# Early x sums, a slot table for the Sinkhorn iterations and an expert-major product, in an attention and mixture-of-experts kernel

## The chip, the cores and the metric

The kernel runs on one core of one Trainium2 chip. The metric is the device time of one execution in microseconds (us). A core has five engines with instruction queues of their own: TensorE (PE; its weight loads are listed as PEld), VectorE (DVE), ScalarE (ACT), GpSimd (POOL) and SyncE (SP), which here only issues DMAs. Each executes its queue in order. An instruction that needs the result of another engine waits for a semaphore, and all that is queued behind it on its engine waits too.

## The reference

```python
k_p, q_p = phi(k), phi(q)      # relu times cos and sin of the position
kv = einsum('bhsf,bhsd->bhfd', k_p, v); z = k_p.sum(2)
x = (q_p @ kv) / (q_p . z + 1e-6)          # 8 batches x 576 rows -> [4608, 512]
P = exp(x @ w_gate)                        # [4608, 8 experts]
for _ in range(8):                         # Sinkhorn
    P /= P.sum(1, keepdims=True) + 1e-9
    P /= P.sum(0, keepdims=True) + 1e-9
    P *= N / E
for e in range(8):
    out += P[:, e:e+1] * (relu(x @ w1[e]) @ w2[e])   # w1 512 x 1024, w2 1024 x 512
```

## The kernel before

**Attention and expert 0, blocks 0 to 6.** x is kept transposed in SBUF as `xT` (128 partitions, 4 slabs of 128 features, 4608 tokens, 16 bit). Expert 0 is computed plainly in blocks of 512 tokens. A block has 16 slots (`NS`): in slots 0 to 7 `ffn1` makes one 128-feature slice of the hidden layer (4 matmuls on PE, relu on ACT), in slots 8 to 15 `ffn2` makes half of a 128-row output tile (4 matmuls; ACT or DVE then copies the tile into the accumulators `acc`). Beside block j the attention of batch j+1 is made: a hand-written list (`todo`, filled by `at(block, slot, ...)`, L587 to L728) says after which slot each step is issued. In block 6 those are `sums` (slot 0), `denominators` (3), `gates` (5) and `attend` (6, 8, 10, 12) of batch 7. `attend` multiplies on DVE into `xT`; `den` and `hl` are the denominators on DVE.

**Blocks 7 and 8** (L1096 to L1121). Attention is over, its pools are closed and their SBUF is used again (weights `wB` of expert 1, hidden layer `H`, `S`, `T` tiles). `gates` of the last batch (L1110) completes the table `P_tok` (128 partitions, 36 token groups, 8 experts, f32). From here on DVE runs the Sinkhorn iterations, a generator (`sinkhorn`, L1022) that `balanced(n)` (L1057) moves on by n steps. Each iteration has five steps: row sums `rs` and their reciprocal `rr`; P_tok times rr and the column sums `colp`; two of the weight sums `T` of expert 1; a matmul of colp with ones, the **Sinkhorn product** (it sums over partitions; the profile's `copied_ps<-colp,ones_all`), and further weight sums; reciprocal `t` and the scaling of P_tok. Block 8 makes its `ffn1` only; its output tiles are left to the unit that follows.

**Experts 1 to 7** use a Strassen-Winograd scheme (7 products for a 2x2 block matrix). Tokens are cut into 6 units of 2 x 384; `group` (L867) makes one slice of the hidden layer of a unit from 7 products of two matmuls each (0.33 us a product) in the PSUM banks X (`h_ps`), Y (`copied_ps`) and Z (`p7_ps`). ACT copies X to Y and takes snapshots u2 and u4 of X; DVE adds them to Z with `add_relu` (L853, in the trace CUSTOM_DVE_ANT_0). The last product of a group is put off into the next group (`late`). Each group calls `fill()` seven times between its products. In the first unit (e = 1, n = 0) the fill is `start_fill` (L1146): it adds pieces of block 8's output tiles (two matmuls) and `balanced` steps. Two matmuls called marks (L1014) enclose this unit: the profile's `copied_ps<-xT`, at 188.79 us and 209.97 us. After it the gates' P values are final, ACT and POOL scale the accumulators, and from then on the fill is the second layer of the unit before.

**x sums.** The scheme needs sums of x blocks for each unit: `x_sums(n)` (L803), four DVE instructions of 128x768 in place S1, S2, S4 and a part of `xT` itself. The three S tiles are also saved to DRAM by SP (L814, `x_saved`), and later experts load them again (`x_again`, L816). Units 0 and 1 are made in blocks 7 and 8, one instruction after a slot (L1112 to L1116).

**Order.** During all of this DVE, ACT and PE execute in written order (`InOrder`, L101). SP and POOL execute in the order in which their instructions were placed.

Of the kernel before, what the change touches and what calls it, by code (L numbers as in the profile page):

```python
# [25 lines left out]
def kernel(  # L26
# [128 lines left out]
    def ffn2(hT, w, c0, g, y_ps, fts):  # L155

        for ft in fts:
            te.matmul(
                out=y_ps,
                lhsT=hT[:, ft, c0 : c0 + P],  # L160
                rhs=w[1][:, ft, :],
                start=(ft == 0),
                stop=(ft == FT - 1),
            )
        if FT - 1 in fts:

            if g % 2 == 0 or g < (B - 1) * TCH // P:
                se.copy(out=acc(g), in_=y_ps)
            else:
                ve.tensor_copy(out=acc(g), in_=y_ps)  # L170

    def store(g, cols=slice(0, Dm), queues=(nc.sync, nc.sync)):
        for half, queue in enumerate(queues):
            w_ = 2 * g + half
            b, c = w_ // C, w_ % C
            rows = out[b * S : (b + 1) * S].rearrange("(p c) d -> p c d", c=C)
            queue.dma_start(
                out=rows[:, c, cols], in_=acc(g)[half * HP : (half + 1) * HP, cols]
            )

    with ExitStack() as p1:
        ld = p1.enter_context(tc.tile_pool(name="ld", bufs=4))
# [404 lines left out]
        def at(block, slot, fn, *args):  # L587
            todo.setdefault((block, slot), []).append((fn, args))
# [62 lines left out]
        for j in range(B):  # L651
# [70 lines left out]
            if j == 1:  # L722
                for name in "qkv":
                    for half in range(2):
                        at(j, 12, load, b + 2, half, name, True)
            elif j and b + 2 < B:
                for half in range(2):
                    at(j, 11 + half, load, b + 2, half, "qkv", True)  # L728
        y_pss = {}
        for j in range(B - 1):  # L730
            if j:
# [34 lines left out]

    NT = N // 2
    TU = 3 * P  # L770
    NU = NT // TU
    KH = KT // 2
    FH = FT // 2
    UG = TU // P
    DH = Dm // 2
    w_next = load_weights(wB, 1)

    H = hB.tile([P, 2, FT, 2 * TU], F16, name="H")
# [12 lines left out]
    Y = ps_k.tile([P, TCH], FP32, name="copied_ps")  # L791
    Z = ps_k.tile([P, TCH], FP32, name="p7_ps")

    def x_part(half, kh, n):
        t0 = half * NT + n * TU
        return xT[:, kh * KH : (kh + 1) * KH, t0 : t0 + TU]

    x_saved = dram.tile([NU, 3, P, KH * TU], F16, name="x_saved")

    def x_tiles():  # L800
        return [s2_pool.tile([P, KH, TU], F16, name=name) for name in ("S1", "S2", "S4")]

    def x_sums(n, ts):  # L803

        a11, a12, a21, a22 = (x_part(i, j, n) for i in range(2) for j in range(2))
        s1, s2, s4 = (t[:] for t in ts)
        for out_, in0, in1, op in (
            (s1, a21, a22, ALU.add), (s2, s1, a11, ALU.subtract),
            (s4, a12, s2, ALU.subtract), (a21, a11, a21, ALU.subtract),
        ):  # L810
            ve.tensor_tensor(out=out_, in0=in0, in1=in1, op=op)
            yield
        for i, t in enumerate(ts):
            nc.sync.dma_start(out=x_saved[n, i], in_=t[:].rearrange("p k t -> p (k t)"))  # L814

    def x_again(n, ts):  # L816
        for i, t in enumerate(ts):
            nc.sync.dma_start(out=t[:].rearrange("p k t -> p (k t)"), in_=x_saved[n, i])
# [203 lines left out]
    def sinkhorn():  # L1022

        total = W2[:, 0:E]
        for it in range(8):
            rs = sk_pool.tile([P, NG], FP32, name="rs")
            ve.reduce_sum(out=rs[:], in_=P_tok[:], axis=AX.X)
            rr = sk_pool.tile([P, NG], FP32, name="rr")
            ve.reciprocal(out=rr[:], in_=rs[:])
            yield  # L1030
            ve.tensor_tensor(
                out=P_tok[:], in0=P_tok[:],
                in1=rr[:].unsqueeze(2).to_broadcast([P, NG, E]), op=ALU.mult,
            )
            colp = sk_pool.tile([P, E], FP32, name="colp")
            ve.reduce_sum(
                out=colp[:], in_=P_tok[:].rearrange("p c e -> p e c"), axis=AX.X
            )
            yield
            for step in tw_steps[it][:2]:  # L1040
                step()
            yield
            te.matmul(out=total, lhsT=ones_all[:], rhs=colp[:], start=True, stop=True)
            for step in tw_steps[it][2:]:
                step()
            yield
            t2 = sk_pool.tile([P, E], FP32, name="t2")
            ve.reciprocal(out=t2[:], in_=total)
            ve.scalar_tensor_tensor(
                out=P_tok[:], in0=P_tok[:],  # L1050
                scalar=float(N) / float(E) / (XS if it == 7 else 1.0),
                in1=t2[:].unsqueeze(1).to_broadcast([P, NG, E]),
                op0=ALU.mult, op1=ALU.mult,
            )
            yield

    def balanced(steps):  # L1057
        for _ in range(steps):
            next(balance, None)
# [26 lines left out]

    balance = sinkhorn()

    tws, tw_steps = [], [[] for _ in range(8)]
    for i in range(FH):  # L1090
        tw, tw_steps[1 + i] = w1_steps(w_next, i)
        tws.append(tw)
    xs_first = [x_tiles() for _ in range(2)]
    xs_next = xs_first[0]
    sums_x = x_sums(0, xs_next)
    for j in range(B - 1, NJ):  # L1096
        hT = next_h()
        tiles = dealt(
            hT, w0, [(ts * P, j * TCH // P + ts) for ts in range(TCH // P)],
            2 if j < NJ - 1 else 4,  # L1100
        )
        for slot in range(NS):
            if slot < FT:
                ffn1(hT, w0, j, [slot])
            elif j < NJ - 1:
                next(tiles)
            else:
                break
            if j == B - 1 and slot == 0:
                gates(B - 1, Z[:])  # L1110
            if j == B - 1 and slot:
                next(sums_x, None)  # L1112
            if j == NJ - 1:
                if slot == 0:
                    sums_x = x_sums(1, xs_first[1])
                next(sums_x, None)  # L1116
            since = (j - B + 1) * NS + slot - 5
            if since == -4:
                balanced(3)
            elif since >= 0 and since % 5 < 2:  # L1120
                balanced((1, 4)[since % 5])  # L1121


    OFFSETS = {"P1": 0, "P2": 3, "P7": 4, "P6": 5, "P4": 8, "P5": 9, "P3": 13}
# [21 lines left out]
    def start_fill():  # L1146

        nonlocal k_fill
        if k_fill % 7 in (0, 2, 3, 5):
            next(tiles, None)  # L1150
        if k_fill % 6 != 1:
            balanced(1)
        k_fill += 1

    def pair_fill():
# [11 lines left out]
    for e in range(1, E):  # L1167
        if e == 2:
            se = nc.scalar
        w = w_next  # L1170
        for n in range(NU):
            hT = next_h()
            xs = xs_next
            for i in range(FH):
                group(hT, tws[i], xs, n, i, start_fill if e == 1 and n == 0 else pair_fill)
                m = (n + 1) % NU
                if e == 1 and m:

                    if n == 0:
                        xs_next = xs_first[1]  # L1180
                        continue
                    if i == 0:
                        xs_next = x_tiles()
                        sums_x = x_sums(m, xs_next)
                    next(sums_x)
                    if i == FH - 1:
                        next(sums_x, None)
                elif i == 1:
                    xs_next = x_tiles()
                    if not (e == E - 1 and m == 0):  # L1190
                        x_again(m, xs_next)

                if e > 1 and n == 0 and i == 0:
                    tws[FH - 1] = w1_sums(w, FH - 1)
                if e + 1 < E and n == NU - 1:
                    if i:
                        tws[i - 1] = w1_sums(w_next, i - 1)
                    else:
                        w2_first(w_next)
            if e == 1 and n == 0:  # L1200
                k_fill = 0
                for _ in tiles:
                    pass
                for _ in balance:
                    pass
                mark(W2[:])
                w2_first(w)
                for _ in range(2):
                    gate(ungated.pop(0), nc.gpsimd)
                ve = nc.vector  # L1210
            if n == 0 and e + 1 < E:
                w_next = new_weights(wA if e % 2 else wB)
                load_w1(w_next, e + 1, 1)
            if n == 2 and e + 1 < E:
                load_w2(w_next, e + 1, 1)
            add_pairs(hT, e, w, n)
# [36 lines left out]
```

The softmax here doesn't subtract the row's maximum and nothing guards it: scores larger than these inputs give would overflow.

## Time and profile before

| what | us |
|---|---|
| median of 6 runs | 981.71 (980.59 to 983.95) |
| profiled execution, whole | 981.78 |
| its span, first to last instruction | 980.1 |
| PE, DVE, ACT busy | 964.5, 806.9, 564.4 |
| a slot of `ffn1` or `ffn2`, from start to start | 0.87 |
| `rs`, `rr`, P_tok times rr, `colp`, `t`, scaling (one each) | 0.45, 0.38, 0.46, 0.67, 0.20, 0.46 |
| one instruction of x sums | 0.55 |
| one weight sum T | 0.28 |
| first Sinkhorn product, last one | 172.15, 204.01 |

All times within the execution count from the start of the span. A busy time is from the start to the end of an instruction. Matmuls overlap: two of them at 128x384 are listed with 0.49 us, and the next pair starts 0.33 us after them. DVE instructions overlap a little too, when one does not need the other: an x sum of 0.55 us is followed 0.47 us after its start. The clock granted to PE was 0.999 of full speed.

### The profile page before, as it was taken

The numbers are of one execution on the slowest core, as the hardware profiler recorded it, in microseconds if no ns is written. First come the engines' busy times: TensorE is split into PE (matmuls) and PEld (weight loads), VectorE is DVE, ScalarE is ACT, GpSimd is POOL, SyncE is SP. The second block draws the span as 40 slices with busy tenths as digits, with TensorE's granted clock in tenths as the row PEclk, the third lists the DMA queues.
The fourth block names the chain that finished last, engine by engine and source line by source line (L and its number), as shares of the span: only waits on it lengthen the run. The fifth ranks groups of instructions, "written<-read, shape, count | busy, mean of one in ns | idle before, by whom it ended". The sixth has DMA issues, their size and how long they took to land.

```text
span 980.1 us, 20237 instructions
## 1 busy us (share of the span) xinstructions
PE 964.5 (98%) x7855; PEld 673.9 (69%) x7855; DVE 806.9 (82%) x1833; ACT 564.4 (58%) x1262; POOL 60.7 (6%) x82
## 2 busy tenths in 40 slices
PE   9999999999999999999999999999999999999997
PEld 6544454457777777777777777777777777777775
DVE  6767774888988888988888888988888888988887
ACT  5766655467776555555555555555555555555551
POOL 6231110010000000000000000000000000000001
PEclk9999999999999999999999999999999999999999
DMA  9999885330113400223103401223103401104435
GB/s 164 183 147 178 149 143 95 79 73 25 43 32 68 92 26 25 64 57 66 49 25 70 91 25 32 61 56 69 42 25 76 85 25 35 40 26 120 127 88 128
DMA packets 80336, 73.54 MB, mean 75 GB/s; under 512 B 33264, under 2 KB 72176, under 8 KB 80240
## 3 DMA queue, kind: packets, MB, share of 16 engines
q0 software_dynamic: 27232, 30.94, 20.3%
q1 hardware_dynamic: 52768, 41.06, 16.9%
q8 instruction: 61, 1.00, 0.4%
q14 instruction: 35, 0.29, 0.1%
q10 hardware_dynamic: 240, 0.26, 0.1%
HBM read 83.12 MB, written 12.98 MB: 98 GB/s over the span
## 4 chain that ended last, share of the span: by engine, by line
PE 88%; DMA 5%; DVE 3%; issue 2%; ACT 1%; POOL 1%; POOLq 0%; ACTq 0%; SPq 0%
PE rows_ps L109 33%; PE h_ps L109 26%; PE p_ps L109 11%; PE copied_ps L109 11%; PE y_ps L109 4%; PE small_ps L109 3%; DMA k_ld<-in_k_dram 1%; DMA w1e<-in_moe_w_dram 1%; DMA w2e<-in_moe_w_dram 1%; DMA acc_hi<-q_p 1%; DVE P_tok L109 1%; DVE colp L109 0%; POOL q_ld L202 0%; DVE rs L109 0%; DVE acc_hi L926 0%
## 5 line engine op out<-in xcount | busy, mean ns | idle before, releaser
L926 DVE SCALAR_TENSOR_TENSOR acc_lo<-rows_ps,P_tok,acc_lo 128x512 f32<-128x512 f32 (+1 forms) x322 | 203.2, 639 | 75.0 <-PE rows_ps L109 74.9
L109 PEld LDWEIGHTS <-H 128*128 128x128 f16 x2080 | 203.0, 98 | 82.6 <-issue 1.2
L862 ACT CAST u<-h_ps 128x384 f16<-128x384 f32 x288 | 137.6, 478 | 131.2 <-PE h_ps L109 131.2
L109 PEld LDWEIGHTS <-w1e 128*128 128x128 f16 x1632 | 157.3, 98 | 67.4 <-issue 5.7
L856 DVE CUSTOM_DVE_ANT_0 H<-p_ps,u 128x384 f16<-128x384 f32 x329 | 180.9, 550 | 6.5 <-PE p_ps L109 6.5
L109 PEld LDWEIGHTS <-hs 128*128 128x128 f16 x1500 | 146.5, 98 | 56.2
L109 PE MATMUL h_ps<-S,w1e 128*128 128x384 f16 x672 | 164.2, 326 | 0.7 <-ACT u L109 0.6
L109 PE MATMUL p_ps<-xT,T 128*128 128x384 f16 x672 | 164.1, 326 | 0.1
L109 PE MATMUL rows_ps<-V,H 128*128 128x256 f16 x1000 | 150.0, 273 | 0.7 <-DVE acc_hi L926 0.7
L109 PE MATMUL rows_ps<-w2e,hs 128*128 128x256 f16 x1000 | 150.0, 273 | 0.0
L109 PE MATMUL h_ps<-xT,w1e 128*128 128x384 f16 (+1 forms) x616 | 149.4, 350 | 0.1
L894 ACT ACTIVATE H<-h_ps 128x384 f16<-128x384 f32 x144 | 70.6, 490 | 95.1 <-PE h_ps L109 95.1
L109 PEld LDWEIGHTS <-T 128*128 128x128 f16 x1008 | 98.4, 98 | 29.9 <-issue 3.2
L109 PE MATMUL rows_ps<-w2e,H 128*128 128x256 f16 (+1 forms) x568 | 92.3, 285 | 0.0
L875 ACT COPY copied_ps<-h_ps 128x384 f32<-128x384 f32 x144 | 67.5, 469 | 35.3 <-PE h_ps L109 35.3
L885 ACT ACTIVATE H<-copied_ps 128x384 f16<-128x384 f32 x144 | 70.8, 492 | 20.4 <-PE copied_ps L109 20.4
L109 PE MATMUL h_ps<-S,T 128*128 128x384 f16 x336 | 81.8, 325 | 0.3 <-ACT copied_ps L109 0.3
L109 PE MATMUL copied_ps<-xT,w1e 128*128 128x384 f16 x336 | 82.1, 326 | 0.0
L109 PE MATMUL copied_ps<-w2e,H 128*128 128x256 f16 x504 | 75.5, 272 | 0.0
L109 PE MATMUL rows_ps<-V,hs 128*128 128x256 f16 x500 | 75.0, 273 | 0.0
L926 DVE SCALAR_TENSOR_TENSOR acc_lo<-copied_ps,P_tok,acc_lo 128x256 f32<-128x256 f32 x126 | 60.0, 476 | 0.4
L926 DVE SCALAR_TENSOR_TENSOR acc_hi<-rows_ps,P_tok,acc_hi 128x512 f32<-128x512 f32 (+1 forms) x56 | 41.3, 737 | 20.5 <-PE rows_ps L109 19.7
(145 smaller groups left out, 948.2 us busy)
## 6 DMA issues: line engine op xcount, KB each, us to landing
S<-x_saved SPq DMA_DIRECT2D x108, 192.0 KB, 2.3
out_dram<-acc_lo SPq DMA_DIRECT2D x62, 128.0 KB, 2.4
w1e<-in_moe_w_dram POOLq DMA_DIRECT2D x7, 1024.0 KB, 8.7
w2e<-in_moe_w_dram POOLq DMA_DIRECT2D x7, 1024.0 KB, 9.8
q_ld<-in_q_dram POOLq DMA_DIRECT2D x16, 288.0 KB, 6.5
k_ld<-in_k_dram POOLq DMA_DIRECT2D x16, 288.0 KB, 8.4
v_ld<-in_v_dram POOLq DMA_DIRECT2D x16, 288.0 KB, 9.7
x_saved<-S SPq DMA_DIRECT2D x18, 192.0 KB, 1.9
```

The costliest lines, as they stand in the source:

```text
L109: i = getattr(self.engine, name)(*args, **kwargs)
L856: latest = ve._custom_dve(TENSOR_ADD_SAT, out=out, in0=ps[:, 0:TU], in1=t[:], s0=FP32_MAX, s1=0.0)
L862: se.copy(out=t[:], in_=ps[:, 0:TU])
L875: se.copy(out=Y[:, 0:TU], in_=X[:, 0:TU])
L885: se.activation(out=h11, in_=Y[:, 0:TU], func=AF.Relu)
L894: se.activation(out=h12, in_=X[:, 0:TU], func=AF.Relu)
L926: ve.scalar_tensor_tensor(out=a, in0=rows, scalar=P_tok[:, g, self.e : self.e + 1], in1=a, op0=ALU.mult, op1=ALU.add,)
```

## The change

1. **x sums of units 0 and 1** are made in block 6, after slot 1 and slot 8, into tiles of the pool of `k_p`, which are free by then (`x_sums_early`). SP saves them to `x_saved`; the S tiles of units 0 and 1 are then loaded from there (`x_again`) when the attention's pools are closed. `x_sums` and the numbers that it needs move up in the file.
2. **Slots.** The steps of the Sinkhorn generator are issued by a table of slots: in blocks 7 and 8 three after slot 1 and five after each of the slots 4, 8, 13, 17 and 22 (counted on from block 7), and in the first unit by a table of the fill's number. Before, it was three after slot 1, one and four after every fifth slot from 5 and the one after it, and one in five of six fills of the unit. So five Sinkhorn products, not four, lie in blocks 7 and 8, and three in the unit. The sixteen weight sums are dealt out 2, 3, 4, 3, 4 to iterations 0 to 4 (before: four each to iterations 1 to 4).
3. **Expert-major product.** P_tok times rr is written into a table `P_exp` with experts outermost (a step of 36 words from expert to expert); `colp` then sums adjacent words; the scaling reads `P_exp` in order and writes `P_tok` in steps of 8 words.
4. **Copies.** The output tiles 29 and 31 (block 7) are copied by ACT, not DVE.

The number of matmuls is the same. DVE has two copies less, ACT two more; SP issues six loads more.

```diff
-            if g % 2 == 0 or g < (B - 1) * TCH // P:
+            if g % 2 == 0 or g < B * TCH // P:
                 se.copy(out=acc(g), in_=y_ps)
...
+        def x_sums_early(n):
+            ts = [kp_pool.tile([P, C, 2, D], F16, name="k_p") for _ in range(3)]
+            for _ in x_sums(n, [
+                t[:].rearrange("p c a d -> p (c a d)")[:, 0 : KH * TU].rearrange(
+                    "p (k t) -> p k t", k=KH
+                ) for t in ts
+            ]):
+                pass
+
+        for n in range(2):
+            at(B - 2, (1, 8)[n], x_sums_early, n)
...
         total = W2[:, 0:E]
+        P_exp = t_pool.tile([P, E, NG], FP32, name="P_exp")
...
             ve.tensor_tensor(
-                out=P_tok[:], in0=P_tok[:],
+                out=P_exp[:].rearrange("p e c -> p c e"), in0=P_tok[:],
                 in1=rr[:].unsqueeze(2).to_broadcast([P, NG, E]), op=ALU.mult,
             )
             colp = sk_pool.tile([P, E], FP32, name="colp")
-            ve.reduce_sum(
-                out=colp[:], in_=P_tok[:].rearrange("p c e -> p e c"), axis=AX.X
-            )
+            ve.reduce_sum(out=colp[:], in_=P_exp[:], axis=AX.X)
...
             ve.scalar_tensor_tensor(
-                out=P_tok[:], in0=P_tok[:],
+                out=P_tok[:].rearrange("p c e -> p e c"), in0=P_exp[:],
                 scalar=float(N) / float(E) / (XS if it == 7 else 1.0),
-                in1=t2[:].unsqueeze(1).to_broadcast([P, NG, E]),
+                in1=t2[:].unsqueeze(2).to_broadcast([P, E, NG]),
...
-    tws, tw_steps = [], [[] for _ in range(8)]
+    tws, steps_left = [], []
     for i in range(FH):
-        tw, tw_steps[1 + i] = w1_steps(w_next, i)
+        tw, steps = w1_steps(w_next, i)
         tws.append(tw)
+        steps_left += steps
+    tw_steps = [[steps_left.pop(0) for _ in range(n)] for n in (2, 3, 4, 3, 4, 0, 0, 0)]
     xs_first = [x_tiles() for _ in range(2)]
     xs_next = xs_first[0]
-    sums_x = x_sums(0, xs_next)
+    for n in range(2):
+        x_again(n, xs_first[n])
...
-            if j == B - 1 and slot:
-                next(sums_x, None)
-            if j == NJ - 1:
-                if slot == 0:
-                    sums_x = x_sums(1, xs_first[1])
-                next(sums_x, None)
-            since = (j - B + 1) * NS + slot - 5
-            if since == -4:
-                balanced(3)
-            elif since >= 0 and since % 5 < 2:
-                balanced((1, 4)[since % 5])
+            balanced({1: 3, 4: 5, 8: 5, 13: 5, 17: 5, 22: 5}.get((j - B + 1) * NS + slot, 0))
...
-        if k_fill % 6 != 1:
-            balanced(1)
+        balanced({3: 1, 4: 1, 5: 1, 6: 2, 11: 1, 12: 1, 13: 1, 14: 2, 19: 1, 20: 1}.get(k_fill, 0))
         k_fill += 1
```

More of the change, by code (lines that the diff above doesn't have):

```diff
@@ L179, in store, with x_part, x_sums @@
             )
+    NT = N // 2
+    TU = 3 * P
+    NU = NT // TU
+    KH = KT // 2
+    FH = FT // 2
+    UG = TU // P
+    DH = Dm // 2
+    def x_part(half, kh, n):
+        t0 = half * NT + n * TU
+        return xT[:, kh * KH : (kh + 1) * KH, t0 : t0 + TU]
+    x_saved = dram.tile([NU, 3, P, KH * TU], F16, name="x_saved")
+    def x_sums(n, ts):
+        a11, a12, a21, a22 = (x_part(i, j, n) for i in range(2) for j in range(2))
+        s1, s2, s4 = ts
+        for out_, in0, in1, op in (
+            (s1, a21, a22, ALU.add), (s2, s1, a11, ALU.subtract),
+            (s4, a12, s2, ALU.subtract), (a21, a11, a21, ALU.subtract),
+        ):
+            ve.tensor_tensor(out=out_, in0=in0, in1=in1, op=op)
+            yield
+        for i, t in enumerate(ts):
+            nc.sync.dma_start(out=x_saved[n, i], in_=t.rearrange("p k t -> p (k t)"))
     with ExitStack() as p1:
@@ L759 @@
     hs_pool = ctx.enter_context(tc.tile_pool(name="hs_pool", bufs=2))
[L769 to L775, printed above, removed]
     w_next = load_weights(wB, 1)
@@ L792 @@
     Z = ps_k.tile([P, TCH], FP32, name="p7_ps")
[L794 to L798, printed above, removed]
     def x_tiles():
         return [s2_pool.tile([P, KH, TU], F16, name=name) for name in ("S1", "S2", "S4")]
[L803 to L814, printed above, removed]
     def x_again(n, ts):
@@ L1183 @@
                         xs_next = x_tiles()
-                        sums_x = x_sums(m, xs_next)
+                        sums_x = x_sums(m, [t[:] for t in xs_next])
                     next(sums_x)
```

## The prediction

> **What bounds it now.** I read the page's busy shares and chain first, then the busy time by stage, then in the worst stage who waits for whom.
>
> ```profile
> PE 964.5 (98%) x7855; PEld 673.9 (69%) x7855; DVE 806.9 (82%) x1833; ACT 564.4 (58%) x1262; POOL 60.7 (6%) x82
> ...
> PE 88%; DMA 5%; DVE 3%; issue 2%; ACT 1%; POOL 1%; POOLq 0%; ACTq 0%; SPq 0%
> ```
>
> PE is the bound; the 3% that the chain gives DVE must lie in one place. The table of stages (length, busy time of PE, PEld, DVE, ACT, POOL) shows where:
>
> ```profile
> 160.00:180.00 20.00, 20.00 (x123) 9.67 (x121) 11.17 (x27) 9.70 (x19) 0.00 (x0) 1.00 0.18 45
> 180.00:200.00 20.00, 17.72 (x91) 8.43 (x90) 17.99 (x48) 9.64 (x19) 0.75 (x1) 1.00 0.39 82
> 200.00:220.00 20.00, 18.37 (x112) 10.72 (x111) 16.51 (x37) 14.48 (x31) 4.07 (x3) 1.00 0.45 83
> 220.00:240.00 20.00, 19.97 (x153) 14.76 (x152) 18.32 (x40) 14.46 (x32) 0.00 (x0) 1.00 0.08 30
> ```
>
> From 180 to 220 us PE is idle 2.28 + 1.63 = 3.9 us while DVE is near full. The waits of PE there (total, times, longest):
>
> ```profile
> PE copied_ps L109 <- DVE colp L109: 3.0, 4, 1.2
> PE h_ps L109 <- ACT u L109: 0.6, 2, 0.3
> PE h_ps L109 <- ACT copied_ps L109: 0.3, 1, 0.3
> ```
>
> Four of the eight Sinkhorn products come too early for their column sums. The chain of waits at the largest (start, us, what):
>
> ```profile
> 188.51 0.47 DVE P_tok L109
> ...
> 189.00 0.46 DVE rs L109
> ...
> 189.49 0.39 DVE rr L109
> ...
> 189.91 0.47 DVE P_tok L109
> ...
> 190.40 0.67 DVE colp L109
> ```
>
> So the stage pays for the DVE chain rs, rr, multiply, colp. It ran late since, between 177.81 and 188.3, DVE also did two copies of PE rows (0.60 each from start to next start; the first came after 1.60 us idle, with t queued behind it) and four sums of x (0.47 to 0.58 each).
>
> **The ceiling.** Between the two marks (188.79 and 209.97) PE takes 21.18 us. Its work, from start to start in the timeline: 27 products of 0.326 (8.80), 16 row pieces of 0.434 (6.94), one mark 0.21, and four Sinkhorn products of 0.24 (0.12 when none is waited for, as at 172.32): 16.9. The gaps 1.36, 0.47, 0.92, 0.90 before Sinkhorn products and 0.20, 0.45 before products that wait for ACT make 4.3. At most some 5 us can be won, 0.5% of the time.
>
> **x sums moved to block 6.** Each unit is four DVE instructions, 0.47 + 0.58 + 0.48 + 0.55 = 2.1 us. Their cover there:
>
> ```profile
> 152.93 0.35 DVE L109 TENSOR_SCALAR den<-small_ps 96x192 f32<-96x192 f32 x1 [2.79 <-PE small_ps L109]
> ...
> 161.59 0.82 DVE L109 TENSOR_TENSOR xT<-small_ps,rb 128x384 f16<-128x384 f32 x2 [1.63 <-ACT rb L109]
> ```
>
> Unit 0 stands ahead of den in an idle stretch of 2.79: hidden (without it up to 2.1, one for one, through den, hl and attend). Unit 1 stands ahead of the row at 161.59, in 1.63 of idle: that row goes 0.4 later, its second half is done at 162.9, and PE wants its bank at 163.50: hidden. PE cost 0. New on SP's queue: unit 0's three saves, three loads behind PE's numerators of 159.05, then unit 1's saves, issued from 160.6 to 161.7, and its loads. Loads are needed at 190 and 206. But ACT's first H of block 7 (167.54) now also waits for unit 1's saves, whose tiles it overwrites; the exp of the gates is queued behind it, then rs. Two h_ps banks and the slack of the first colp allow a landing until about 168.2. With idle DMA engines a save lands in 1.9: 163.6. With the expert's weights still loading (w2e issued 149.40, landing 13.2 later; engines full from 152), it adds: three saves 1.6 us of all engines (1.07 for two at 187 to 189), three loads 3.0 (2.0 for two at 282 to 286), three saves 1.6, so 162.6 + 6.2 = 168.8 at worst. Cost 0 to 0.6; I take 0.
>
> **Copies to ACT.** Two row copies of block 7 (0.58 on ACT) fall into ACT idle time of 3.00 and 2.44 us. DVE is rid of 1.2 us and of the wait before t.
>
> **The strided table.** Per iteration the rows of before are these:
>
> ```profile
> L109 DVE TENSOR_REDUCE colp<-P_tok 128x8 f32<-128x288 f32 x8 | 5.3, 669 | 0.3
> ...
> L109 DVE TENSOR_TENSOR P_tok<-P_tok,rr 128x288 f32<-128x288 f32 x8 | 3.7, 458 | 0.3
> L109 DVE SCALAR_TENSOR_TENSOR P_tok<-P_tok,t 128x288 f32<-128x288 f32 x8 | 3.7, 458 | 0.3
> L109 DVE TENSOR_REDUCE rs<-P_tok 128x36 f32<-128x288 f32 x8 | 3.6, 452 | 3.2 <-ACT P_tok L109 3.0
> ```
>
> The same 288 values cost 0.452 read in order and 0.669 read in steps of 8 words: 0.217 for stepping. After, colp reads in order (0.452 expected), but two writes step (36 and 8 words per element). No row has a stepped f32 write. Below: nothing, since the broadcasts of rr step by zero and cost nothing. Above: the two cs_half copies (18 elements, read and write stepped) took 0.175 and 0.309 against 0.143 for an ordered copy of 32, so 1.8 to 9.2 ns per element, or 0.5 to 2.6 per write. I take the nearest row, 0.217 per write (0.675 each), so an iteration gets 0.217 longer, not shorter.
>
> The Trainium skill (Vector Engine (DVE) Microarchitecture Reference, Measured stream behaviour on trn2, its access granule) speaks against this edit: full rate needs pairs of adjacent words, sources that step by 72 or 152 words cost 1.75 ns per element against 1.05, and a destination alone stepping by 24 words 2.5 ns. For the source the trace agrees (0.217 over 288 elements is 0.75 ns more each); no run here shows the destination. By 2.5 a write would take about 0.88, and the sum below would be 2.0 us instead of 3.1, an estimate from that page.
>
> **The new places.** A round trip, product to next column sums, from starts in the timeline: product to t 0.33, t 0.23, scaling 0.70, rs 0.49, rr 0.42, multiply 0.70, colp 0.48: 3.35. Blocks 7 and 8 now hold five products after slots 4, 8, 13, 17, 22. PE's slots take 0.866, so there are 3.58 us (four slots and a product) or 4.45. Products stand at 171.45, 175.03, 179.49, 183.08, 187.53, sums are ready 0.2 to 1.1 earlier: no wait. The sixteen weight sums (0.2 to 0.3 each) fit into DVE's waits for products, and the weights landed at 156.9, before the first at 170.4. PE saves 0.3 here: before, four products took 0.12, 0.12, 0.24 and 0.24 and waited 0.05 and 0.13; after, five take 0.60.
>
> In the unit between the marks three products are left, at 191.31, 195.95 and 202.0, each with its sums ready: 0.36 instead of 0.96. Work is then 16.3. Stalls left: with the product gone from its place, the second product of each group meets ACT's copy of Y (0.30, 0.18); ACT's gates later 0.06 + 0.12 + 0.30; and one new wait. Behind the seventh product's t stand scaling, rs, rr, multiply and colp of the last iteration, and only then the add that frees Z. DVE reaches t at 197.75 (it waits for u4 at 196.68 and a row copy first) and that add ends at 201.23; PE wants Z at 200.11: 1.14 lost. Sum 2.1; the stretch takes 18.4 instead of 21.18, 2.75 less. With 0.3 from the blocks it is **3.1 us**. Worked in the same way the kernel before has its second mark at 210.07 (trace 209.97), so I trust it to some 0.3. Afterwards PE is again at 19.97 of 20, and the gain stays.
>
> The profiled execution took 981.78 (span 980.1 and 1.7 around it), the median 981.71: they are the same here. 981.78 - 3.1 = **978.7**.
>
> **Rivals.** (a) Stepped writes are free: the Z wait shrinks by 0.43, 978.3. For: the write may be buffered; against: stepped reads are not. (b) A stepped write costs 0.9 to 1.0: trips of 3.8 to 4.0 no longer fit four slots, PE stalls at 175 and 183, the Z wait grows to 1.6 and more: gain 0.7 to 2, about 980.3. The lower cs_half copy (0.5 more) says so. (c) Unit 1's saves land after 168.2: some 1.0 with the exp behind it, 979.7. For: full DMA engines until 162.6; against: 4.6 us of margin in an idle queue. (d) Slower: the table's writes dearer than 1.05 each, where the longer trips eat the whole 3.1; at 1.2 it loses 2.2 us, at 1.3 3.7: 985.5. It needs 2.1 ns more per element than in order, nearly three times the stepped read's 0.75; only the higher cs_half copy says so. (e) The gain is lost elsewhere, or the edits do nothing: 981.7. Against: the instruction orders show each move, and no later stage has slack to lose it in.
>
> **Numbers.** Forecast 50%, own range 978.0 to 979.4; (a) 12%, (b) 18%, (c) 10%, (d) 6%, (e) 4%. 0.2% is what a measurement here tells from no change, so faster means under 979.75: the forecast nearly whole, (a), half of (c) and a bit of (b): 0.71. Slower: (d) and a little: 0.07. The range, 977.7 to 981.0, takes in the forecast, (a), (c) and nearly all of (b).
>
> **What would show it.** Right: no PE wait on colp from 170 to 210; colp at 0.45, both table instructions near 0.67; one PE wait of about 1.1 before a p_ps product near 200; the second mark near 207; block 6 as long as before. Wrong: table instructions near 0.46 or above 0.85; ACT's first H after 168.2; den or attend later in block 6.

## The result and the profile after

The changed kernel takes **979.03 us** (median of 22 runs, 977.97 to 980.82), the one before 981.28 (44 runs, so 0.4 under the 981.71 of the six runs that the prediction started from): ratio 0.9977, 95% interval 0.9971 to 0.9983, so 1.7 to 2.8 us less. The profiled execution took 978.91 (span 977.2), 2.87 less than the 981.78 of before; 0.93 of these have nothing to do with the change, as the account below shows.

The page's busy line and its chain by engine, of the changed kernel:

```profile
PE 963.6 (99%) x7855; PEld 674.4 (69%) x7855; DVE 807.6 (83%) x1831; ACT 565.5 (58%) x1264; POOL 60.7 (6%) x82
...
PE 89%; DMA 5%; issue 2%; DVE 2%; POOL 1%; ACT 0%; ACTq 0%; POOLq 0%; SPq 0%; DVEq 0%
```

PE is the bound as before; DVE's part of the chain fell from 3% to 2%. The stages (length, busy time of PE, PEld, DVE, ACT, POOL, clock, DMA share, GB/s):

```profile
160.00:180.00 20.00, 19.44 (x120) 9.48 (x118) 12.69 (x34) 9.67 (x19) 0.00 (x0) 1.00 0.42 116
180.00:200.00 20.00, 19.78 (x105) 10.15 (x104) 16.63 (x40) 11.88 (x24) 0.76 (x1) 1.00 0.32 53
200.00:220.00 20.00, 18.22 (x118) 11.44 (x118) 17.22 (x37) 15.37 (x33) 4.07 (x3) 1.00 0.45 83
220.00:240.00 20.00, 19.97 (x154) 14.71 (x151) 18.05 (x41) 14.44 (x32) 0.00 (x0) 1.00 0.09 32
```

The idle time of 2.28 us from 180 to 200 is down to 0.22, but 0.56 has appeared from 160 to 180, where PE had none, and from 200 to 220 PE is idle as much as before (1.78; 1.63). PE's waits between 150 and 222 us (total, times, longest) name both:

```profile
PE p_ps L109 <- DVE H L109: 1.0, 1, 1.0
PE h_ps L109 <- ACT H L109: 0.6, 1, 0.6
PE h_ps L109 <- ACT u L109: 0.3, 1, 0.3
PE h_ps L109 <- ACT copied_ps L109: 0.3, 1, 0.3
```

No wait on `colp` is left. In its place stand the predicted wait for Z (1.0) and one of 0.6 for ACT's `H`. That second one comes from a DMA; ACT's timeline (start, us, what, idle before and its end) shows the first `H` of block 7:

```profile
167.84 0.60 ACT L109 ACTIVATE H<-h_ps 128x512 f16<-128x512 f32 x1 [1.52 <-DMA x_saved<-k_p]
```

It waits until unit 1's saves have left the tiles that `H` takes over. The listed 0.56 counts from the modelled end of the matmul before; from start to start, against the gates, PE's matmul at 168.49 comes 0.73 later than in the kernel before. DVE's groups from 160 to 212 us (busy, mean ns | idle before) show the table's prices:

```profile
L109 DVE SCALAR_TENSOR_TENSOR P_tok<-P_exp,t 128x288 f32<-128x288 f32 x8 | 5.4, 679 | 0.3
L109 DVE TENSOR_TENSOR P_exp<-P_tok,rr 128x288 f32<-128x288 f32 x8 | 5.4, 670 | 0.3
L109 DVE TENSOR_REDUCE colp<-P_exp 128x8 f32<-128x288 f32 x8 | 3.6, 453 | 0.3
```

Each stepped write takes 0.21 to 0.22 us more than the ordered one (458 ns), `colp` 0.216 less (669): an iteration is 0.21 longer.

**The account.** The PE matmuls are counted through, from 0: number 1700 of 7855 lies in block 6, at 152.22 us before and 151.29 after. Unit 0's early sums begin at 149.12, shortly ahead of it, but from number 1000 to number 1700 both kernels take 64.67 us. From number 2500 on the order is the same in all versions. The loading phase ahead of number 1000 takes 84.8 to 89.7 us after the first matmul in the fourteen traces, without any pattern: in the changed kernel 0.93 less than in the kernel before. So versions are compared by the **stretch** from PE's first matmul of the gates in block 7 to the second mark, and by the time from matmul 1700 to matmul 7000. Each comes from one trace per version; from number 1000 to the gates, a part that the versions hardly touch, all fourteen traces have 79.78 or 79.79 us. Parts of the change's effect, in us against before:

| part | before | after | difference |
|---|---|---|---|
| gates (167.34; 166.40) to first mark (188.79; 188.17) | 21.45 | 21.77 | +0.32 |
| first mark to second (209.97; 206.62) | 21.18 | 18.45 | -2.73 |
| a product on Z soon after (211.46 in the changed kernel) | | | +0.15 |
| one matmul at 676.04 | | | +0.28 |
| all from matmul 1700 to 7000 | 711.38 | 709.37 | -2.01 |

The first row is 0.73 lost at 168.49 and 0.41 won by the products. The 2.0 agree with the interval of the medians, 1.7 to 2.8. Of the 3.1 predicted, 1.1 is missing.

### The profile page after: what moved, and what is told of

It reads as the page before. It is cut to its first block, busy times and chain, and to the rows that moved or that the text cites. A ratio compares the mean times of both kernels' runs of the same rounds, so it can differ in the third digit from the quotient of the medians.

```text
span 977.2 us, 20250 instructions
## 1 busy us (share of the span) xinstructions
PE 963.6 (99%) x7855; PEld 674.4 (69%) x7855; DVE 807.6 (83%) x1831; ACT 565.5 (58%) x1264; POOL 60.7 (6%) x82
## 4 chain that ended last, share of the span: by engine, by line
PE 89%; DMA 5%; issue 2%; DVE 2%; POOL 1%; ACT 0%; ACTq 0%; POOLq 0%; SPq 0%; DVEq 0%
PE rows_ps L109 34%; PE h_ps L109 27%; PE p_ps L109 11%; PE copied_ps L109 11%; PE y_ps L109 4%; PE small_ps L109 3%; DMA k_ld<-in_k_dram 1%; DMA w2e<-in_moe_w_dram 1%; DMA w1e<-in_moe_w_dram 1%; DMA acc_hi<-q_p 1%; DMA x_saved<-k_p 1%; POOL q_ld L229 0%; DVE acc_hi L939 0%; POOL hs_last L954 0%; DMA out_dram<-acc_lo 0%
```

## Experiments

The versions in one table (stretch; its two parts, gates to first mark and between the marks; the time from matmul 1700 to 7000 against before; median against the runs of before on the same chip; ratio with its 95% interval). Intervals of neighbouring versions overlap, so verdicts on the smaller effects rest on the stretch and the waits.

| version | stretch | parts | 1700 to 7000 | median | ratio |
|---|---|---|---|---|---|
| before | 42.63 | 21.45, 21.18 | 0 | | |
| after | 40.22 | 21.77, 18.45 | -2.01 | -2.25 | 0.9977 (0.9971 to 0.9983) |
| e6_table_only | 43.79 | 21.88, 21.91 | +1.19 | +1.53 | 1.0014 (1.0005 to 1.0022) |
| p1_sums_only | 41.31 | 21.86, 19.45 | -1.34 | -1.66 | 0.9992 (0.9980 to 1.0004) |
| p2_slots_only | 40.71 | 21.66, 19.05 | -1.84 | -1.72 | 0.9981 (0.9972 to 0.9990) |
| e1_row_major | 40.01 | 21.76, 18.25 | -2.26 | -2.07 | 0.9980 (0.9971 to 0.9989) |
| e2_old_slots | 41.17 | 21.25, 19.92 | -1.25 | -0.93 | 0.9986 (0.9974 to 0.9997) |
| e3_sums_late | 41.15 | 21.68, 19.47 | -1.11 | -1.33 | 0.9991 (0.9982 to 1.0000) |
| e8_copies_dve | 40.22 | 21.76, 18.46 | -2.28 | -2.26 | 0.9972 (0.9960 to 0.9983) |
| e4_saves_first | 39.49 | 21.04, 18.45 | -2.75 | -2.98 | 0.9970 (0.9959 to 0.9981) |
| e7_z_first | 39.25 | 21.65, 17.60 | -2.97 | -3.01 | 0.9968 (0.9955 to 0.9982) |
| c1_all | 38.44 | 21.04, 17.40 | -3.76 | -3.30 | 0.9964 (0.9952 to 0.9977) |
| d1_y_pieces | 37.81 | 21.04, 16.77 | -4.46 | -4.51 | 0.9959 (0.9947 to 0.9971) |
| d7_copies_dve | 37.81 | 21.04, 16.77 | -4.71 | -4.98 | 0.9951 (0.9937 to 0.9964) |

The theory (T1): the gain comes from DVE's queue being rid of the x sums and from the new places of the products; the table costs; the missing part went to the saves. Its rivals are named in each expectation.

### Undoing one part at a time

**The table in token-major order (e1_row_major).**

```diff
-                out=P_exp[:].rearrange("p e c -> p c e"), in0=P_tok[:],
+                out=P_tok[:], in0=P_tok[:],
...
-            ve.reduce_sum(out=colp[:], in_=P_exp[:], axis=AX.X)
+            ve.reduce_sum(
+                out=colp[:], in_=P_tok[:].rearrange("p c e -> p e c"), axis=AX.X
+            )
...
-                out=P_tok[:].rearrange("p c e -> p e c"), in0=P_exp[:],
+                out=P_tok[:], in0=P_tok[:],
...
-                in1=t2[:].unsqueeze(2).to_broadcast([P, E, NG]),
+                in1=t2[:].unsqueeze(1).to_broadcast([P, NG, E]),
```

> The changed kernel with the third part of the change undone (the table keeps its token-major order, nothing is written in steps, the column sums read in steps of 8 words again). The measure is the stretch from PE's first matmul of the last batch's gates (166.40 in the changed kernel) to the second mark (206.62): 40.22 us in the changed kernel, 42.63 in the one before. T1 (the gain comes from DVE's queue being freed and from the new places of the products; the table order costs about 0.2 us an iteration): an iteration gets 0.21 us shorter (0.458 + 0.669 + 0.458 instead of 0.670 + 0.453 + 0.679), no wait of PE on the column sums comes back, and the wait of PE for H before Z's product shrinks by 0.2: the stretch 40.0, the time 0.2 below the changed kernel. T3 (the expert-major order is what gains, since the product waits for column sums that now take 0.45): waits of PE on the column sums come back, stretch 41 or more, time 0.8 or more above the changed kernel.

Measured: 40.01, no wait on `colp`, the wait for Z 0.8 instead of 1.0:

```profile
PE p_ps L109 <- DVE H L109: 0.8, 1, 0.8
```

T1 holds, T3 falls: the expert-major order costs this kernel 0.2 us, all of it in the wait for Z. The median (979.30) can't show so little.

**The old places (e2_old_slots).**

```diff
-    tw_steps = [[steps_left.pop(0) for _ in range(n)] for n in (2, 3, 4, 3, 4, 0, 0, 0)]
+    tw_steps = [[steps_left.pop(0) for _ in range(n)] for n in (0, 4, 4, 4, 4, 0, 0, 0)]
...
-            balanced({1: 3, 4: 5, 8: 5, 13: 5, 17: 5, 22: 5}.get((j - B + 1) * NS + slot, 0))
+            since = (j - B + 1) * NS + slot - 5
+            if since == -4:
+                balanced(3)
+            elif since >= 0 and since % 5 < 2:
+                balanced((1, 4)[since % 5])
...
-        balanced({3: 1, 4: 1, 5: 1, 6: 2, 11: 1, 12: 1, 13: 1, 14: 2, 19: 1, 20: 1}.get(k_fill, 0))
+        if k_fill % 6 != 1:
+            balanced(1)
```

> The changed kernel with the second part undone: the Sinkhorn steps stand in the places of the kernel before, and the weight sums are dealt 0, 4, 4, 4, 4 again; early sums, table and copies stay. T1 (both the places and the freed DVE queue are needed): PE waits on the column sums before three products of the unit, about 0.3, 1.1 and 0.9 us, by a walk through the engines' orders with the durations of the trace: stretch 41.6 (changed kernel 40.22, before 42.63), time 1.4 above the changed kernel, still 0.8 to 1.1 below the kernel before. T2 (the slots alone give the gain, the moved sums nothing): stretch as before, 42.6, time 981.3.

Measured: 41.17, three products of the unit wait 0.18, 0.95 and 0.72:

```profile
PE copied_ps L109 <- DVE colp L109: 1.8, 3, 0.9
```

T1's places are right, its waits 0.1 to 0.2 too long. The stall behind the saves was 0.18 here: the gates came 0.37 later in the span than in the changed kernel, while ACT's first `H` started at 167.83, as there (167.84). T2 falls: with the old places the kernel still gains 1.5 on the stretch.

**The sums in blocks 7 and 8 (e3_sums_late).**

```diff
-        for n in range(2):
-            at(B - 2, (1, 8)[n], x_sums_early, n)
...
-    for n in range(2):
-        x_again(n, xs_first[n])
+    sums_x = x_sums(0, [t[:] for t in xs_next])
...
+            if j == B - 1 and slot:
+                next(sums_x, None)
+            if j == NJ - 1:
+                if slot == 0:
+                    sums_x = x_sums(1, [t[:] for t in xs_first[1]])
+                next(sums_x, None)
```

> The changed kernel with the first part undone: the x sums of units 0 and 1 are made in blocks 7 and 8 again, one instruction after a slot; slots, table and copies stay. T1: PE waits on the column sums twice, about 0.45 and 0.9 us in blocks 7 and 8, since DVE has 4.2 us more to do there; the stall of 0.56 us that PE has at 168.49 before h_ps (ACT's first H waits for unit 1's saves) is gone. Stretch 41.0 (changed kernel 40.22), time 0.8 above the changed kernel. T2 (slots alone): no wait on the column sums, and the stall gone, so stretch 39.5 and time 0.6 below the changed kernel.

Measured: 41.15, two waits on `colp` (0.34 and 0.74), no stall behind saves:

```profile
PE copied_ps L109 <- DVE colp L109: 1.1, 2, 0.7
```

T1 holds, but for a place: the second wait, at 193.80, comes after the first mark (190.13), so in the unit and not in block 8.

**The copies by DVE (e8_copies_dve).**

```diff
-            if g % 2 == 0 or g < B * TCH // P:
+            if g % 2 == 0 or g < (B - 1) * TCH // P:
```

> The changed kernel with the fourth part undone: tiles 29 and 31 are copied by DVE again. T1 (once the x sums are gone from blocks 7 and 8, DVE has room there): no wait of PE on the column sums, stretch 40.2, time the same as the changed kernel within 0.2. Rival T6 (the two copies are what made the products of iterations 3 to 5 late, as the 1.60 us of idle time before the first one in the kernel before suggests): waits on the column sums of 0.5 or more come back, stretch 40.7 or more.

Measured: 40.22, the same waits. In the stretch the fourth part is worth nothing; T6 falls. What it does elsewhere is told below.

### One part alone

**The table alone (e6_table_only)**: the third part's lines in the kernel before.

> The kernel before with the third part of the change alone (expert-major product between the two steps of an iteration). T1: an iteration is 0.21 us longer (0.670 + 0.453 + 0.679 instead of 0.458 + 0.669 + 0.458), and in the kernel before DVE sets the pace from the fourth product on, so the waits on the column sums grow from 3.0 to about 4.0: stretch 43.6 (before 42.63), time 0.8 to 1.0 above the kernel before. T3 (the expert-major order gains, as colp gets shorter): stretch 42.0 or less, time at least 0.6 below the kernel before.

Measured: 43.79, +1.16. PE's waits in the kernel before with that table:

```profile
PE copied_ps L109 <- DVE colp L109: 4.0, 6, 1.4
```

Six waits and 4.0 us instead of four and 3.0. So the same 0.21 per iteration costs 1.2 us where DVE sets the pace, and 0.2 where it doesn't.

**The sums alone and the slots alone (p1_sums_only, p2_slots_only)**: the first and the second part's lines in the kernel before.

> The kernel before with the first part alone: x sums of units 0 and 1 made in block 6, saved, loaded again; old places of the Sinkhorn steps, token-major table, tiles 29 and 31 by DVE. By a walk through the engines' orders (T1: the sums' 4.2 us of DVE work and the places of the products remove the same waits, so either alone gets most of the gain): waits on the column sums 0.2 in the blocks and 0.8 and 0.9 before the last two products of the unit, plus 0.2 to 0.6 for H behind the saves; stretch 40.8 to 41.1 (before 42.63, changed kernel 40.22), time 1.5 to 1.8 below the kernel before. Rival T2 (slots alone matter): 42.6 and no change of the time. Rival T7 (the parts add up: the version without the second part showed -1.46, the table alone +1.16): 40.0.

> The kernel before with the second part alone: the table of slots and the dealing of the weight sums; x sums in blocks 7 and 8, token-major table, tiles 29 and 31 by DVE. T1: waits on the column sums of 0.2 in the blocks and 0.65 at the first product of the unit, the wait of 0.9 before Z's product, no stall behind saves: stretch 40.6, time 2.0 below the kernel before, so that the first part of the change on top of it is worth 0 to 0.4 as long as its saves stall PE. T7 (the parts add up): 40.0. Rival T8 (the places only pay once DVE is rid of the x sums): 42 or more.

Measured: 41.31 and 40.71. Each alone wins most: 1.3 and 1.9, 3.2 together; both with the token-major table (e1_row_major) win 2.6. They are paid partly for the same waits, so T7 and T8 fall. For the sums alone the forecast was 0.2 too low: two waits of 0.74 on `colp` came as expected in place (0.8 and 0.9 expected), the 0.2 in the blocks did not, and PE waited 0.5 for `H`; the rest was not followed. For the slots alone the waits were 0.14 and 0.54 on `colp` (0.2 and 0.65 expected) and 0.80 before Z's product (0.9).

### Where the missing gain went

**The saves ahead of the loads (e4_saves_first).**

```diff
-            nc.sync.dma_start(out=x_saved[n, i], in_=t.rearrange("p k t -> p (k t)"))
+            saves[n] = nc.sync.dma_start(out=x_saved[n, i], in_=t.rearrange("p k t -> p (k t)"))
...
-            nc.sync.dma_start(out=t[:].rearrange("p k t -> p (k t)"), in_=x_saved[n, i])
+            i = nc.sync.dma_start(out=t[:].rearrange("p k t -> p (k t)"), in_=x_saved[n, i])
+            if first:
+                not_before(saves[1], i)
```

> The changed kernel with one order changed on SP's queue: unit 0's three loads from DRAM are issued after unit 1's three saves, not before them. T1 (ACT's first H of block 7 waits for unit 1's saves, which stand behind unit 0's loads and land at about 167.8): if the loads are what delays the saves, the saves land 1.4 us or more earlier, the stall of 0.56 us at 168.49 goes, the stretch is 39.5 to 39.7 and the time 0.5 to 0.7 below the changed kernel. Rival T4 (the saves are late because the DMA engines are full with the weights of expert 0 and 1's loads that POOL issued, whatever stands ahead on SP): the saves land at 167 or later, ACT's first H starts within 0.3 us of 167.84, stretch 40.0 to 40.2, time the same.

SP's timeline from 157 to 168 us (start of the first, us to the end of the last), first of the changed kernel, then of this version:

```profile
158.15 2.65 SPq L831 DMA_DIRECT2D S<-x_saved  x3
160.84 1.43 SPq L206 DMA_DIRECT2D x_saved<-k_p  x3
166.33 1.31 SPq L831 DMA_DIRECT2D S<-x_saved  x3
```

```profile
159.77 1.50 SPq L208 DMA_DIRECT2D x_saved<-k_p  x3
161.44 4.66 SPq L833 DMA_DIRECT2D S<-x_saved  x6
```

Unit 1's saves are issued 1.07 us earlier, and ACT's first `H` starts at 166.85 and waits for PE alone. The stretch is 39.49: all of the 0.73 is won back. T4 falls as the cause of the stall: the weights that POOL loads fill the DMA engines all the same in this version (the DMA share is 0.95 or more up to 166), so that these saves too take 4.8 to 5.1 us to land, and yet they arrive in time.

What held the saves up in the changed kernel shows in the waits of SP's queue:

```profile
SPq L831 <- DMA x_saved<-k_p: 10.8, 4, 5.8
```

The last of these four waits is of unit 1's own loads. Unit 0's loads (L831) read what unit 0's saves write, and each waits on SP until its save has landed. The third save landed at 160.46, 9.57 us after its issue; the third load was issued at 160.48, and unit 1's first save, queued behind it, at 160.84. The saves then landed at 166.31 to 167.30, after the loads ahead of them (163.76 to 165.79). In e4_saves_first they landed at 164.82 to 165.72, ahead of the loads (166.22 on). Counted from the gates, the last save was issued 1.08 us earlier and landed 1.83 earlier.

The Trainium skill states an order for what has been issued (DMA: Bandwidth & Descriptors, Queues, rings and completion order): on each DMA engine the descriptors of one queue are taken in the order of their ring. The landings of this pair of runs agree with it.

**Z's add ahead of the last iteration (e7_z_first).**

```diff
-        balanced({3: 1, 4: 1, 5: 1, 6: 2, 11: 1, 12: 1, 13: 1, 14: 2, 19: 1, 20: 1}.get(k_fill, 0))
+        balanced({3: 1, 4: 1, 5: 1, 6: 2, 11: 1, 12: 1, 13: 1, 15: 2, 19: 1, 20: 1}.get(k_fill, 0))
```

> The changed kernel with two of the Sinkhorn steps (scaling and row sums; multiply and column sums stand with them) of the last iteration issued one fill later, after fill 15 instead of 14, so that DVE makes the add that frees the bank Z before them. T1 (the wait of 1.0 us that PE has before Z's product at 200.95 is DVE's queue: the add stands behind the last iteration): that wait goes, in its place PE waits 0.2 to 0.3 for the column sums of the last product; stretch from the gates to the second mark 39.4 (changed kernel 40.22), time 0.8 below the changed kernel. Rival T5 (the add is late because ACT's snapshot u or PE's own product before it is late): the wait stays near 1.0, stretch 40.2, time the same.

DVE's timeline in the changed kernel (PE starts the product on Z at 200.95 after 1.0 of waiting), then in this version:

```profile
198.87 0.38 DVE L109 RECIPROCAL rr<-rs 128x36 f32<-128x36 f32 x1
199.28 0.66 DVE L109 TENSOR_TENSOR P_exp<-P_tok,rr 128x288 f32<-128x288 f32 x1
199.98 0.45 DVE L109 TENSOR_REDUCE colp<-P_exp 128x8 f32<-128x288 f32 x1
200.35 0.55 DVE L109 CUSTOM_DVE_ANT_0 H<-p_ps,u 128x384 f16<-128x384 f32 x1
```

```profile
198.04 0.38 DVE L109 RECIPROCAL rr<-rs 128x36 f32<-128x36 f32 x1
198.33 0.50 DVE L109 CUSTOM_DVE_ANT_0 H<-p_ps,u 128x384 f16<-128x384 f32 x1
198.74 0.66 DVE L109 TENSOR_TENSOR P_exp<-P_tok,rr 128x288 f32<-128x288 f32 x1
199.44 0.45 DVE L109 TENSOR_REDUCE colp<-P_exp 128x8 f32<-128x288 f32 x1
```

The add (CUSTOM_DVE_ANT_0) now stands ahead of the multiply and `colp`. Between the marks 17.60 instead of 18.45, and the wait for Z is gone: T1 holds, T5 falls. No wait of 0.2 on `colp` is listed in its place; the last product's time in the timeline grew from 0.28 to 0.39 us. So 0.85 of the stretch's gain of 0.97 is the edit's; the other 0.12 lie ahead of the first mark, where the saves landed a little earlier in this trace.

### A better version

**Three edits together (c1_all)**: e4_saves_first, e7_z_first and the token-major table.

> The changed kernel with three edits together: unit 0's loads behind unit 1's saves on SP's queue, the last iteration's steps after fill 15, and the token-major table. T1: the stall before h_ps at 168.49 (0.56) and the wait before Z's product (1.0) are both gone, and with the shorter iterations (0.21) no wait on the column sums over 0.1 takes their place: stretch 38.6 to 38.8 (changed kernel 40.22, before 42.63), time 1.4 to 1.6 below the changed kernel and some 3.8 below the kernel before. Rival: what one edit wins is lost in the next wait (DVE's other work behind the later iteration, ACT's copies of Y), stretch 39.2 or more, no better than the reordered queue alone (39.49).

Measured: 38.44, 0.2 better than expected; the gains add up (0.73, 0.85 and 0.2).

**The row pieces moved (d1_y_pieces)**: c1_all, and in the unit's fill:

```diff
-        if k_fill % 7 in (0, 2, 3, 5):
+        if k_fill % 7 in (0, 1, 3, 5):
...
-        balanced({3: 1, 4: 1, 5: 1, 6: 2, 11: 1, 12: 1, 13: 1, 15: 2, 19: 1, 20: 1}.get(k_fill, 0))
+        balanced({3: 1, 4: 1, 5: 1, 6: 2, 11: 1, 12: 1, 13: 1, 15: 2, 20: 2}.get(k_fill, 0))
```

> The changed kernel with the three edits of the combined version (unit 0's loads behind unit 1's saves, the last iteration's steps after fill 15, token-major table), and besides: the pieces of block 8's output tiles in the unit stand in fills 0, 1, 3, 5 of each seven, not 0, 2, 3, 5, and the last two Sinkhorn steps after fill 20 together. T1 (what is left between the marks is PE's second product of a group that comes too early for ACT's copy of X to Y, 0.30 and 0.18, since the Sinkhorn product has gone from that place): these gaps go, and no new gap over 0.2 appears behind the snapshots; stretch 37.8 to 38.0 (combined version 38.44, changed kernel 40.22, before 42.63), time 0.5 below the combined version, some 4.3 below the kernel before. Rival: PE then waits as long for the snapshots u2 and u4, stretch 38.4 or more.

Measured: 37.81, 16.77 between the marks. T1 holds: the pieces now cover ACT's copy of X to Y. Of the 0.63 won between the marks, 0.29 and 0.20 come from the two places that were forecast (0.30 and 0.18); the rest lies where the last Sinkhorn product moved.

**The same with the copies by DVE (d7_copies_dve)**: the edit of e8_copies_dve on top.

> The best version so far (saves first, last iteration's steps after fill 15, token-major table, pieces of the output tiles in fills 0, 1, 3, 5) with tiles 29 and 31 copied by DVE as in the kernel before. What it is to tell apart: in all eight versions in which ACT copies these two tiles, one matmul of a much later stage (h_ps before x S, at 676.04 in the changed kernel) starts 0.28 us late behind ACT's copy of X to Y, and in none of the five versions in which DVE copies them. T9 (the two copies on ACT cause it, through ACT's instruction stream being two longer from then on): the 0.28 at that place is gone, stretch 37.8 as before it, so the later part of the profile is 0.28 earlier against the gates. T10 (it is chance, or comes from the other parts): the 0.28 stays. In the stretch itself nothing: DVE has room for 1.2 us in block 7. Time 0.3 below the version with ACT's copies, too small for the medians to show alone.

What led to it: past matmul 2500 all versions keep step to 0.1 us, but for one matmul, number 5589, which comes 0.28 late in every version whose tiles 29 and 31 ACT copies, and in no other. ACT's timeline there, of the changed kernel, then of e8_copies_dve:

```profile
675.52 0.46 ACT L888 COPY copied_ps<-h_ps 128x384 f32<-128x384 f32 x1 [0.61 <-PE h_ps L109]
```

```profile
676.18 0.46 ACT L888 COPY copied_ps<-h_ps 128x384 f32<-128x384 f32 x1 [0.33 <-PE h_ps L109]
```

The product that ACT copies starts at 674.66 and 675.60, so the copy starts 0.86 and 0.58 after it: 0.28 later with nothing else late, and PE's next product needs the bank. In d7_copies_dve the copy again starts 0.58 after its product (673.72, 674.30) and the 0.28 is gone: T9 holds as far as the tie to ACT's copies goes. How two instructions at 177.60 and 181.19 us do this some 500 us later stays open. In all fourteen traces, with and without the 0.28, an instruction-queue packet starts 0.7 to 1.2 us before that matmul and another 0.1 to 0.5 us after it, so that a code load lies there is no explanation by itself.

This version takes **976.63 us** (5 runs, 976.42 to 977.70; before 981.61 on the same chip), ratio 0.9951 (0.9937 to 0.9964). Its stages:

```profile
160.00:180.00 20.00, 20.00 (x123) 9.82 (x122) 13.82 (x36) 9.24 (x18) 0.00 (x0) 1.00 0.51 130
180.00:200.00 20.00, 20.00 (x110) 10.56 (x109) 16.69 (x42) 11.58 (x23) 0.76 (x1) 1.00 0.31 53
200.00:220.00 20.00, 19.16 (x127) 12.13 (x125) 17.81 (x39) 16.00 (x35) 4.07 (x3) 1.00 0.45 83
```

PE is idle 0.84 us from 160 to 220, where the kernel before had 3.9; by the matmuls 4.7 us are won, near the ceiling of about 5 that the prediction worked out.

## Why the prediction was right, and where it was not

- **The time.** 978.7 was predicted, 979.03 is the median. The sum was too large by more than these 0.3: 3.1 against 2.0 by the matmuls, and 2.25 by the medians. The forecast still came close since it started from 981.78, while the kernel before has a median of 981.28 over 44 runs; that is luck. The profiled execution came close to the forecast (978.91) since its loading happened to be 0.93 shorter.
- **The unit between the marks: right.** 18.4 predicted, 18.45 measured; no wait on `colp`; the wait for Z at 1.0 (1.14 predicted), its cause shown by e7_z_first. The two gaps at ACT's copy to Y came close to the prediction: 0.29 and 0.20 us in c1_all, against 0.30 and 0.18.
- **Blocks 7 and 8: right without the saves.** Five products without a wait, saving 0.3: e4_saves_first has 21.04 up to the first mark against 21.45, 0.41 less. There the products lie 3.59, 8.05, 11.64 and 16.09 after the first, as the places in the prediction do (3.58, 8.04, 11.63, 16.08).
- **The saves: the step that failed.** "With idle DMA engines a save lands in 1.9: 163.6. [...] so 162.6 + 6.2 = 168.8 at worst. Cost 0 to 0.6; I take 0." The last save landed at 167.30, which is 168.24 by the clock of the trace of before: past the 163.6 that was taken and at the 168.2 that the working allowed, and it cost 0.73 of PE's time. Two terms are wrong. First, the landing: the working put unit 0's loads behind a matmul alone, but they wait on SP for unit 0's saves too, and unit 1's saves stand behind them in the queue. Of the six saves the median landing was 6.4 us instead of 1.9, and POOL's two weight loads took 9.7 and 17.0 us instead of 8.2 and 13.2. Second, the working let `H` start with the landing. The trace's records of ACT's queue have seven semaphore instructions ahead of this `H`; the first ends its wait with the last save, the others follow in steps of 0.08 us, and `H` starts at 167.84, 0.54 after the landing, as it does in all six versions that stall here. In e4_saves_first they are done while ACT waits for PE. As an estimate: `H` is 1.24 late against the gates and PE loses 0.73, so 0.51 are free, and an `H` that started with the landing, 0.70 late, would have cost 0.19. With the weights and the loads ahead written down, the upper end was the likelier one. It is rival (c), at about three quarters of its price.
- **The copies: wrong by 0.28, at a place that the prediction had excluded.** "No later stage has slack to lose it in" held for slack, but e8_copies_dve and d7_copies_dve show that the copies on ACT cost 0.28 at 676 us. A further 0.15 is lost at 211.46 in a wait on Z, also after the second mark; e2_old_slots and p1_sums_only, with the old places, don't have it.
- **The table: right.** 0.675 per stepped write was predicted, 0.670 and 0.679 came; `colp` 0.453 (0.452). That it costs rather than helps is shown by e1_row_major (0.2) and e6_table_only (1.2). Rivals (a), (b) and (d) fall with the price. The figure that the prediction took from the Trainium skill (Vector Engine (DVE) Microarchitecture Reference, Measured stream behaviour on trn2), 2.5 ns per element for a destination stepping by 24 words (0.88 a write, an estimate), does not carry over to these steps of 36 and 8 words: the writes cost 0.74 and 0.77 ns per element more than in order.
- **Block 6: right.** From matmul 1000 to the gates 79.79 us before and after. Unit 0's sums end at 151.33, and `den` still waits for PE; unit 1's are followed at once by the row they delay:

```profile
152.00 0.35 DVE L109 TENSOR_SCALAR den<-small_ps 96x192 f32<-96x192 f32 x1 [0.67 <-PE small_ps L109]
...
161.06 0.81 DVE L109 TENSOR_TENSOR xT<-small_ps,rb 128x384 f16<-128x384 f32 x2
```

## What to carry to other kernels

Work moved off a full engine's queue brings its transfers along: put the transfers whose end frees a buffer ahead of those that merely fetch, above all when the fetch itself waits for an earlier transfer in the same queue, and when the working names a loaded queue and other transfers ahead, take the upper bound of their landing. Two edits that shorten the same waits are not paid twice, and the price of a dearer instruction depends on whether its engine sets the pace there (1.2 us and 0.2 us for the same one). After a wait is removed, look one place on in the same queue for what is now late; moving two steps by one fill won 0.85 us.

## What the runs showed of the hardware

- An f32 write of 288 elements in steps of 36 or 8 words takes 0.66 to 0.68 us on DVE, in order 0.458; a read in steps of 8 words 0.669 against 0.452. Reading and writing in steps cost the same, 0.7 to 0.8 ns per element.
- A save of 192 KB from SP's queue that lands in 1.9 us by itself took 6.4 (median of six) beside two weight loads of POOL and other transfers of SP.
- Seven semaphore instructions stand ahead of ACT's first `H` of block 7. Where the first waits for a DMA, the other six follow in steps of 0.08 us, and `H` starts 0.54 us after the landing (six versions). Where the last save landed earlier, `H` starts 0.20 us after the gates, as in the kernel before.
- Two instructions more on ACT at about 180 us came with one copy on ACT starting 0.28 us late 500 us later, at the same instruction in eight of eight versions that have them and in none of six that don't. The cause is open.
